# Attention with a mixture of experts on one core: five experts with an early block instead of four, gates by groups of query blocks, scaling by token tile, and weight maxima loaded expert by expert

## The chip, the cores and the metric

One core of a Trainium2 chip runs the whole program. The metric is the device time of one execution in microseconds (us); the kernel before is given by the median of three runs, and a profile of one further execution, with the start and length of every instruction, is what the prediction is argued from. PE is TensorE, DVE VectorE, ACT ScalarE, POOL GpSimd, SP SyncE, whose queue issues most transfers.

## The reference

Causal attention with a window of 128 over 8 batches, 8 heads, 576 positions and head size 64; its output, 4608 tokens of 512 numbers, goes through a mixture of 8 experts with noisy top-2 routing.

```python
mask = (rel >= 0) & (rel < window)                  # window = 128
scores = np.where(mask, scale * q @ k.T + slopes * -abs(rel), -1e9)
x = (softmax(scores) @ v)                           # rows: (batch, position), 512 wide
noisy = x @ w_gate + np.log1p(np.exp(x @ w_noise)) * noise
top2 = np.argpartition(-noisy, 2, axis=1)[:, :2]    # two experts per token, softmax weights
for e in range(8):
    for k in range(2):
        mask = top2[:, k] == e
        h = np.maximum(x[mask] @ w1[e], 0.0)        # 512 -> 1024
        out[mask] += top2_w[mask, k, None] * (h @ w2[e])   # 1024 -> 512
```

## The kernel before

**Precision.** Attention and the gate are computed in fp32. An expert's product is made of three products of rounded parts: high x high, high x low, low x high. In the first wave of expert blocks the parts are fp32r; in the second they are fp16, for which tokens and weights are first multiplied by a power of two that fits their largest absolute value, and the result is scaled back by `back`.

**Planner.** The order of the instructions on each engine is fixed while the program is written. Strands (Python generators) ask for an engine with an assumed duration and a rank, the due time; a small event simulation (`Order`) gives each engine, whenever it is free in the plan, the waiting step of the lowest rank. `either(a, b, rank, late, ...)` offers a step to ScalarE and, `late` us later, to VectorE. Buffers and PSUM banks are handed round in rings, also by rank. An `Event` holds a strand back in the plan; it is no semaphore of its own on the chip. `move` puts a transfer on SyncE's queue. The assumed durations and offsets at the top (`STAGE`, `LATE`, `GATE`, ...) steer the plan.

**Attention.** For each pair of heads (32) and each group of query blocks (`GROUPS`: blocks 0 and 1, blocks 2 and 3, the half block 4) a `unit` runs scores (L486 and L493), maxima with the bias on VectorE (L511), the exponential on ScalarE (L518), transposes (L530), their copies, and the product with the values (L561), whose result is copied to `xu`. When the four pairs of a batch are done, `rows` starts for each query block a `gate` (logits of gate and noise, L690, then the division by the softmax sums, L694, and the sum over heads, L699, on VectorE) and a `row_major` (L669, L672), which writes the tokens to `xs` in DRAM. `largest_value` takes the maximum of every value tile on VectorE (L455, L458, L459); since a token is a mean of values, one power of two from it (`xsc`) scales all tokens of the second wave.

**Routing.** `route(b)` follows batch by batch, one after the other: best two, their positions within each expert by products with triangular and all-one matrices (L746 to L750), a one-hot list of slots (L784, L790, product L794), and a scatter by GpSimd into the slot lists in DRAM (L870), for which `next_places` (L777) makes the row numbers `line_of`. For batches in `TIGHT` a chain of small steps is one planned step; for the others the last one-hot step may go to GpSimd.

**First wave.** After two batches (`CUTS`), the first 256 slots (`FIRST`) of experts 0 to 3 (`NF`) are filled, and their blocks run in fp32r between the attention steps: `weight` loads 256 KB pieces, casts them to the high part and subtracts for the low part (L988); `tokens` gathers the rows by GpSimd (L1059); `turn_tokens` transposes them; `ups` runs the up products (`mm1`, L1092) of a step (128 of the 1024 hidden columns), `middle` makes relu high part (L1112, L1114) and low part (L1129), `downs` the down products (`mm2`, L1140). The due times of the steps are spread evenly from `FFN0` to `FFN1`. Up products have one PSUM bank of their own (`hb`), shared with the routing's position products, down products two.

**Second wave.** When all units and all routes are done (`over`), attention's buffers are closed and the rest of each expert's slots runs in fp16: two blocks (512, 448) for the experts with a first block, three (512, 384, 320) for the others (`BLOCKS`). The last block of an expert has its down product flipped (L1145), so that the weights are the stationary side, and its result turned (L1200). `result` scales by the gate weight and scatters by GpSimd (L1219). Weights come through `scaled_weight` (L1044, L1048), which needs the expert's power of two; for experts 0 and 1 (`EARLY`) it comes from the rounded weights of the first wave (L992), for experts 2 to 7 `size_of_weights` loads each expert's weights once more in 512 KB pieces through three buffers (`mraw`, L1010) and reduces them (L1011), all six experts from the start of the second wave on, by rank.

After the planned part a loop over overflowing slots follows; the slots hold all tokens here, so it has no pass.

Of the kernel before, what the change touches and what calls it, by code (L numbers as in the profile page):

```python
# [22 lines left out]
NQ = 5  # L23
# [5 lines left out]
NF = 4  # L29
# [12 lines left out]
VALUES_LATE = 4.0  # L42
# [3 lines left out]
PLACES_LATE = 10.0  # L46
# [8 lines left out]
EARLY = 2  # L55
# [152 lines left out]
def attention_moe(ctx: ExitStack, tc: tile.TileContext, qk_, v, w_gate, w_noise, noise, w1, w2,  # L208
# [57 lines left out]
    ltr = ring(ap_, 2, [128, H, 16], F32, "lt")  # L266
# [37 lines left out]
    line_of = const.tile([E * SPAN, 1], I32, name="line_of")  # L304
    am = const.tile([128, 4], F32, name="am")
    mx = const.tile([128, 1], F32, name="mx")
# [3 lines left out]
    xmx = const.tile([128, 1], F32, name="xmx")  # L310
    xex = const.tile([128, 1], I32, name="xex")
    xsc = const.tile([128, 1], I32, name="xsc")
    xback = const.tile([128, 1], I32, name="xback")
    topped = Event()
# [27 lines left out]
    def set_ups():  # L342
# [19 lines left out]
        def columns():  # L362
# [6 lines left out]
            nc.vector.tensor_copy(line_of, first_line)  # L369
# [50 lines left out]
    def all_values():  # L420
        for y in range(2 * B):
# [30 lines left out]

    def largest_value(y, t, rank):
        def most(z, j, c):
            nc.vector.tensor_reduce(am[:, z:z + 1], t[:, j:j + c], axis=AX.XY, op=OP.max, apply_absolute_value=True)  # L455

        def all_():
            nc.vector.tensor_reduce(mx, am[:, 0:3], axis=AX.X, op=OP.max)  # L458
            nc.vector.tensor_tensor(xmx, xmx, mx, op=OP.max)  # L459

        for z, (j, c) in enumerate(((0, 2), (2, 2), (4, 1))):
            yield dve(0.34 if c == 1 else 0.6, rank, lambda: most(z, j, c))
        yield dve(0.14, rank, all_)
        if y == 2 * B - 1:
            spawn(powers_of_tokens())

    def powers_of_tokens():
        rank = FFN1 - 20
        a, wide = yield from of_all(xmx, 1, rank)

        def powers():
            floor_powers(xex, wide)
            nc.vector.tensor_scalar(xsc, xex, -1.0, float(256 << 23), op0=OP.mult, op1=OP.add)
            nc.vector.tensor_scalar(xback, xex, float(-2 << 23), None, op0=OP.add)

        yield dve(0.3, rank, powers)
        put(tb, a)
        put(turn_, 0)
        mark(topped)
# [93 lines left out]
    def unit(u):  # L573
# [45 lines left out]
        if g == NP - 1:  # L619
            spawn(rows(b, gr, t))  # L620
# [858 lines left out]
```

## Time and profile before

| what | value |
|---|---|
| runs | 1229.28, 1231.8, 1232.81 us |
| median | 1231.8 us |
| profiled execution, its own time | 1238.91 us |
| its span, first to last instruction | 1237.1 us |
| mean granted TensorE clock | 0.977 |
| second wave's first up product | at 450.3 us |
| weight pieces of 256 KB / maxima pieces of 512 KB | 192 / 48 loads |
| bytes moved by DMA | 169.13 MB |

A row of the profile's groups gives line, engine, operation, output and inputs with shapes, the count; then busy us of the group and mean ns of one; then the idle time of the engine just ahead of them and what ended it. The busy time of a group is the union of its instructions, so for pipelined products it is less than count times mean. Line numbers are those of the kernel above. A matmul in fp32 is recorded as two instructions.

### The profile page before, as it was taken

What the parts mean: (1) busy time and instruction counts of PE and PEld (TensorE: products, weight loads), DVE (VectorE), ACT (ScalarE), POOL (GpSimd) and SP (SyncE); (2) the same over time, 40 slices, a digit from 0 to 9 for tenths busy, and PEclk for the clock granted to TensorE, in tenths of its full rate; (3) what the DMA queues carried; (4) which work ended last, traced back from release to release, by engine and by line L of the source; (5) the groups of instructions that cost most, each with busy time, mean ns of one, the idle gap of its engine ahead of it and who ended that gap; (6) DMA issues with size and microseconds to landing.
All of it is one profiled execution on the core that took longest, in us unless ns stands there. A gap on an engine that the chain in (4) does not pass through costs nothing.

```text
span 1237.1 us, 20624 instructions
## 1 busy us (share of the span) xinstructions
PE 1165.7 (94%) x7447; PEld 722.2 (58%) x7447; DVE 694.4 (56%) x2108; ACT 518.6 (42%) x1365; POOL 292.3 (24%) x329
## 2 busy tenths in 40 slices
PE   7999799999997898999799999999999999999995
PEld 5776577778786763554454554555664564565552
DVE  7996789799988987665642432522351262242210
ACT  8775477676632352341331432332342251243211
POOL 5000101122224540320311331133221222322211
PEclk9998799999997999999999999999999999999998
DMA  8795445555244797885851651543451363342221
GB/s 266 279 308 192 136 121 162 159 157 131 58 133 125 230 293 244 251 232 163 246 124 31 142 124 25 147 86 61 90 134 30 53 174 61 61 112 43 35 26 22
DMA packets 132470, 169.13 MB, mean 137 GB/s; under 512 B 25360, under 2 KB 85008, under 8 KB 132368
## 3 DMA queue, kind: packets, MB, share of 16 engines
q1 hardware_dynamic: 114448, 127.48, 32.1%
q0 software_dynamic: 17920, 40.33, 17.7%
q8 instruction: 59, 0.97, 0.3%
q14 instruction: 43, 0.35, 0.1%
HBM read 126.38 MB, written 41.40 MB: 136 GB/s over the span
## 4 chain that ended last, share of the span: by engine, by line
PE 69%; DVE 10%; DMA 9%; issue 9%; ACT 2%; POOL 1%; SPq 0%; another core or an unknown queue 0%; POOLq 0%; DVEq 0%; ACTq 0%
PE bank L1092 26%; PE bank L1140 18%; PE bank L1145 8%; PE bank L561 3%; PE bank L530 3%; PE bank L493 3%; DMA raw<-in_w_dram 2%; PE bank L1072 2%; DMA out_dram<-yo,ix 2%; DVE p L511 2%; DMA slots_dram<-listed,line_of 1%; PE bank L690 1%; DVE wam L1011 1%; DMA xg<-xs_dram,ix 1%; DMA out_dram<-yo,ids 1%
## 5 line engine op out<-in xcount | busy, mean ns | idle before, releaser
L1129 DVE SCALAR_TENSOR_TENSOR bhl<-bank,bhh 128x512 f16<-128x512 f32 (+3 forms) x160 | 97.5, 610 | 334.6 <-ACT bhh L1112 320.8
L1219 POOL DMA_INDIRECT out_dram<-yo,ix x72 | 114.0, 1583 | 571.0 <-ACT yo L247 450.1
L1112 ACT ACTIVATE bhh<-bank 128x512 f16<-128x512 f32 (+3 forms) x146 | 78.7, 539 | 395.5 <-PE bank L1092 391.8
L1092 PE MATMUL bank<-bxh,w1hb 128*128 128x512 f16 (+3 forms) x640 | 222.3, 347 | 0.4 <-DMA xg<-xs_dram,ix 0.4
L1092 PE MATMUL bank<-bxl,w1hb 128*128 128x512 f16 (+3 forms) x640 | 222.1, 347 | 0.0
L1092 PE MATMUL bank<-bxh,w1lb 128*128 128x512 f16 (+3 forms) x640 | 222.1, 347 | 0.0
L1092 PEld LDWEIGHTS <-w1hb 128*128 128x128 f16 x1280 | 124.1, 98 | 104.3 <-issue 2.4
L1140 PE MATMUL bank<-w2hb,bhh 128*128 128x512 f16 (+1 forms) x376 | 142.8, 380 | 2.1 <-ACT bhh L1112 2.1
L1140 PE MATMUL bank<-w2hb,bhl 128*128 128x512 f16 (+1 forms) x376 | 142.5, 379 | 1.3 <-DVE bhl L1129 1.1
L1140 PE MATMUL bank<-w2lb,bhh 128*128 128x512 f16 (+1 forms) x376 | 142.5, 379 | 0.0
L518 ACT ACTIVATE p<-p,nm 128x256 f32<-128x256 f32 (+2 forms) x288 | 133.8, 469 | 10.1 <-DVE nm L511 9.5
L1140 PEld LDWEIGHTS <-bhh 128*128 128x128 f16 (+1 forms) x752 | 72.4, 98 | 82.8 <-issue 4.6
L511 DVE CUSTOM_DVE_ANT_0 p<-bank,bias 128x256 f32<-128x256 f32 (+2 forms) x288 | 95.3, 379 | 15.1 <-PE bank L493 10.6
L1092 PEld LDWEIGHTS <-w1lb 128*128 128x128 f16 x640 | 62.6, 98 | 55.0
L1082 DVE SCALAR_TENSOR_TENSOR bxl<-bank,xsc,bxh 128x512 f16<-128x512 f32 x72 | 51.6, 717 | 70.5 <-ACT bxh L247 55.5
L493 PE MATMUL bank<-qk 64*128 64x256 f32 (+1 forms) x512 | 72.0, 394 | 17.3 <-DVE nm L511 12.5
L530 PE MATMUL bank<-ident,p 128*128 128x128 f32 x512 | 83.2, 290 | 3.5 <-DVE pT L251 1.9
L561 PE MATMUL bank<-pT,vraw 128*64 128x128 f32 (+3 forms) x896 | 83.1, 309 | 1.3 <-DVE pT L251 0.7
L1059 POOL DMA_INDIRECT xg<-xs_dram,ix x72 | 72.7, 1009 | 23.9 <-issue 16.2
L1145 PE MATMUL bank<-bhh,w2hb 128*128 128x448 f16 (+1 forms) x224 | 74.5, 332 | 3.7 <-ACT bhh L1112 2.7
L247 ACT ACTIVATE pT<-bank 128x512 f32<-128x512 f32 (+1 forms) x115 | 56.6, 509 | 46.3 <-PE bank L530 41.8
L1145 PE MATMUL bank<-bhl,w2hb 128*128 128x448 f16 (+1 forms) x224 | 74.4, 332 | 1.0 <-DVE bhl L1129 1.0
(220 smaller groups left out, 1968.3 us busy)
## 6 DMA issues: line engine op xcount, KB each, us to landing
raw<-in_w_dram SPq DMA_DIRECT2D x192, 256.0 KB
mraw<-in_w_dram SPq DMA_DIRECT2D x48, 512.0 KB
qk<-in_qk_dram SPq DMA_DIRECT2D x32, 608.0 KB
out_dram<-xg SPq DMA_DIRECT2D x10, 1024.0 KB
vraw<-in_v_dram SPq DMA_DIRECT2D x16, 512.0 KB
xs_dram<-x SPq DMA_DIRECT2D x32, 256.0 KB
vraw<-in_v_dram SPq DMA_DIRECT2D x16, 128.0 KB
xg<-xs_dram,ix POOLq DMA_INDIRECT x72
```

The lines of the kernel that those rows point to most:

```text
L493: nc.tensor.matmul(s[h][:, o:o + c], qk[half, i * 128:i * 128 + 128], qk[half, QW + k0:QW + k0 + c], start=True, stop=True)
L511: nc.vector.tensor_tensor_reduce(out=p[:, z, h, 0:c], in0=s[h][:, o:o + c], in1=bv, scale=-0.125, scalar=3.0e38, op0=OP.add, op1=OP.min, a ...
L518: nc.scalar.activation(pv, pv, AF.Exp, bias=nm[:, z, h:h + 1], scale=-1.0, accum_out=den[:, z, 2 * g + h:2 * g + h + 1])
L530: nc.tensor.transpose(t[:, z], p[:, h, a:a + 128], ident)
L561: nc.tensor.matmul(o[half, o0:o0 + c], t[p0:128, kb, hh:hh + D], w, start=m == 0, stop=m == len(lst) - 1)
L1059: yield pool(1.04, rank, lambda: nc.gpsimd.indirect_dma_start(out=xg[0:r], out_offset=None, in_=xs[0:blk.rows], in_offset=bass.IndirectOff ...
L1092: nc.tensor.matmul(t[:, 0:blk.n], wp[:, c], x[:, c, 0:blk.n], start=c == 0 and z == 0, stop=c == 3 and z == 2)
L1112: nc.scalar.activation(o, i, AF.Relu)
L1129: yield dve(0.07 + c * 0.00104, rank - MIDDLE, lambda: nc.vector.scalar_tensor_tensor(hl[:, 0:c], t[:, 0:c], 0.0, high, op0=OP.max, op1=OP ...
L1140: nc.tensor.matmul(blk.y[j][0:r], h[:, cs], wp, start=f == 0 and m == 0, stop=f == 7 and m == 2)
L1145: nc.tensor.matmul(blk.y[c][:, 0:blk.n], wp[:, c * 128:c * 128 + 128], h[:, 0:blk.n], start=f == 0 and m == 0, stop=f == 7 and m == 2)
L1219: ins = nc.gpsimd.indirect_dma_start(out=out, out_offset=bass.IndirectOffsetOnAxis(ap=blk.ix[0:r, j:j + 1], axis=0), in_=t[0:r], in_offset ...
```

## The change

- `NF` 4 to 5: experts 0 to 4 get a first block of 256 slots; expert 4's second-wave blocks become (512, 448). `FFN0` and `FFN1`, between which the first wave's due times are spread, stay.
- `EARLY` 2 to 1: only expert 0's maxima come from the first wave. For experts 1 to 7 the 512 KB pieces are loaded, each expert's not before, in the plan, the previous expert's first second-wave block begins (`begun`).
- `largest_value`, `powers_of_tokens`, `xsc`, `xback` are gone; instead `fit` takes, for each gathered token tile of the second wave, the maximum per token, a power of two, scales the rows, and puts the inverse into the gate weights.
- `gate` works on a group: the four products have the 32 gate columns as stationary side and up to 256 tokens as moving side, each into 32 partitions of its own; the result is copied to SBUF (`gt`) and transposed back per block; the division and the sum over heads are one instruction each per group.
- `banks`: when all units are done (`attended`), and not the routes too, the two score banks go to the up products and one bank of the value product to the down products. The rest (one bank of `tb`) still waits for `over`.
- The slot list's place columns are ten small instructions with two per-partition operands in place of two large ones, always on VectorE; `line_of` has two buffers.

The diff, cut:

```diff
-NF = 4
+NF = 5
-EARLY = 2
+EARLY = 1
...
-            left["v", y] = 2 * len(GROUPS) + 1
+            left["v", y] = 2 * len(GROUPS)
             mark(valued[y])
-            yield from largest_value(y, t, rank + VALUES_LATE)
-            through(y)
...
-        done = Event(2 * nz)
+        done = Event(nz + 1)
+        spawn(gate(b, blocks, xus[b, gr], den, t, done))
...
-    def gate(b, i, xu, den, t, done):
+    def gate(b, blocks, xu, den, t, done):
...
             for c in range(4):
-                nc.tensor.matmul(a[0:rows, c * 32:c * 32 + 32], xu[:, c], wgn[:, c], start=True, stop=True)
+                nc.tensor.matmul(a[c * 32:c * 32 + 32, 0:c_], wgn[:, c], xu[:, c, 0:c_], start=True, stop=True)
-        yield pe(0.9, rank, logits)
+        yield pe(0.45 if nz == 2 else 0.15, rank, logits)
+        gt = yield (gtr, rank)
+        yield either(*((0.12, 0.13) if nz == 1 else (0.29, 0.33)), rank, LATE[2], lambda e: copy(
+            e, gt[:, 0:c_], a[:, 0:c_]))
...
+                nc.tensor.transpose(a2[0:rows, z * 128:z * 128 + 128], gt[:, z * 128:z * 128 + rows], ident)
...
-            V.tensor_add(line_of, tmp[0:m, 1, 0:1], first_line)
+            V.tensor_add(line_of[(b + 1) % 2], tmp[0:m, 1, 0:1], first_line)
...
+        def which_place(i):
+            for k in range(2):
+                V.tensor_scalar(hot[1][:, 2 * i + k], steps_[:, 0:LINE], d[:, i, k:k + 1], numbers[:, i:i + 1],
+                                op0=OP.is_equal, op1=OP.mult)
...
+    begun = [Event() for _ in range(E)]
     def size_of_weights(rg):
         for e in range(EARLY, E):
             done, rank = Event(8), SIZES[1] + step_of(e)
+            yield begun[e - 1]
...
+    def fit(blk, j, r, xg, rank):
+        m = yield (fitr, rank)
+        big, up_, down = (m[0:r, z:z + 1] for z in range(3))
...
+            V.tensor_mul(blk.gw[0:r, j:j + 1], xg[0:r, DM + blk.e:DM + blk.e + 1], down)
+        yield dve(0.6, rank, lambda: V.tensor_reduce(big, xg[0:r, 0:DM], axis=AX.X, op=OP.max, apply_absolute_value=True))
+        yield dve(0.7, rank, powers)
+        yield either(0.6, 0.6, rank, LATE[6], lambda e: copy(e, xg[0:r, 0:DM], xg[0:r, 0:DM], scale=up_))
...
     def ups(p, steps, ranks):
         for (blk, f), rank in zip(steps, ranks):
             if f == 0:
                 yield blk.ready
+                if p and begun[blk.e].count:
+                    mark(begun[blk.e])
...
+    def banks():
+        yield attended
+        for t in sb.free.pop():
+            put(hbr, t)
+        t = yield (ob, 0)
+        put(yb, t)
...
-        for r in (tb, ob):
-            t = yield (r, 0)
-            put(yb, t)
-        for t in sb.free.pop():
-            put(hbr, t)
+        t = yield (tb, 0)
+        put(yb, t)
```

More of the change, by code (lines that the diff above doesn't have):

```diff
@@ L41 @@
 VALUES = -12.4
-VALUES_LATE = 4.0
 GATE = (-41.8, -83.8)
@@ L303, in attention_moe @@
     tmp = const.tile([128, 2, E], F32, name="tmp")
-    line_of = const.tile([E * SPAN, 1], I32, name="line_of")
-    am = const.tile([128, 4], F32, name="am")
-    mx = const.tile([128, 1], F32, name="mx")
+    line_of = [const.tile([E * SPAN, 1], I32, name=f"line_of{z}") for z in range(2)]
     tops = const.tile([2, 1], F32, name="tops")
@@ L561, in weigh @@
                 nc.tensor.matmul(o[half, o0:o0 + c], t[p0:128, kb, hh:hh + D], w, start=m == 0, stop=m == len(lst) - 1)
-    over = Event(n + B)
+    over, attended = Event(n + B), Event(n)
     groups_ = range(len(GROUPS))
@@ L654, in attention_moe @@
     open_ = [Event() for _ in range(B + 1)]
-    gates = [Event(NQ) for _ in range(B)]
+    gates = [Event(len(GROUPS)) for _ in range(B)]
     routed = [Event() for _ in range(B)]
@@ L679, in row_major @@
         put(xr, x)
-    def gate(b, i, xu, den, t, done):
+    def gate(b, blocks, xu, den, t, done):
         rank = t - GATE[b + 1 in CUTS]
-        rows = 64 if i == 4 else 128
+        nz, i = len(blocks), blocks[0]
+        rows, c_ = (64, 64) if nz == 1 else (128, 256)
         yield set_up
@@ L857, in route @@
         spawn(gates_out(b, rank))
-        for c_, c2, f in hots:
-            if b in TIGHT or f is not number:
-                yield dve(c_, rank, lambda: f("DVE"))
-            else:
-                yield Op((("POOL", c2, rank), ("DVE", c_, rank + PLACES_LATE)), f)
+        yield dve(0.98, rank, which_line)
+        for i in range(NQ):
+            yield dve(0.28, rank, lambda: which_place(i))
         a = yield (tb, rank)
@@ L869, in scatter @@
             nc.gpsimd.memset(pad, 0.0)
-            nc.gpsimd.indirect_dma_start(out=slots, out_offset=bass.IndirectOffsetOnAxis(ap=line_of[:, 0:1], axis=0),
+            nc.gpsimd.indirect_dma_start(out=slots, out_offset=bass.IndirectOffsetOnAxis(ap=line_of[b % 2][:, 0:1], axis=0),
                                          in_=listed, in_offset=None, compute_op=OP.add)
@@ L942, in attention_moe @@
     second, lists2 = [], []
+    fitr = Ring([])
     chunks = {}
@@ L1030, in powers @@
             V.tensor_mul(back[:, e:e + 1], inv[:, 0:1], inv[:, 1:2])
-            V.tensor_mul(back[:, e:e + 1], back[:, e:e + 1], xback.bitcast(F32))
         yield dve(0.4, rank, powers)
@@ L1074, in turn_tokens @@
         yield pe(0.43, rank, turn)
-        yield either(0.16, 0.07, rank, 0.0, lambda e: copy(e, blk.gw[0:r, j:j + 1], xg[0:r, DM + blk.e:DM + blk.e + 1]))
+        if blk not in second:
+            yield either(0.16, 0.07, rank, 0.0, lambda e: copy(e, blk.gw[0:r, j:j + 1], xg[0:r, DM + blk.e:DM + blk.e + 1]))
         put(xgr, xg)
@@ L1259, in second_wave @@
         for z in range(4):
+            put(fitr, more.tile([128, 3], F32, name=f"fit{z}"))
+        for z in range(4):
             put(ixr, more.tile([128, 4], I32, name=f"ix{z}"))
         spawn(size_of_weights(ring(more, 3, [128, 1024], F32, "mraw")))
-        for r in (tb, ob):
-            t = yield (r, 0)
-            put(yb, t)
-        for t in sb.free.pop():
-            put(hbr, t)
+        t = yield (tb, 0)
+        put(yb, t)
         second.extend(Block(e, s0, c, NPAD, rings2) for e in range(E) for s0, c in BLOCKS[e >= NF])
@@ L1381, in attention_moe @@
     steps1 = [(blk, f) for blk in first for f in range(8)]
-    for strand in (loads(), masks(), all_values(), set_ups(), first_wave(), first_tokens(), second_wave(),
+    for strand in (loads(), masks(), all_values(), set_ups(), first_wave(), first_tokens(), banks(), second_wave(),
                    weights(0, lambda e, f: ranks1[8 * e + f] - WEIGHTS), last_weights(), all_powers(),
```

83 lines of the change are left out of this document (30 added, 53 removed).

## The prediction

> **What bounds the kernel now.** I read the page first (span, busy shares), then the stretches of 25 us, then the chain that ended last, and only then single groups and the order of time around the places that the change touches.
>
> ```profile
> span 1237.1 us, 20624 instructions
> PE 1165.7 (94%) x7447; PEld 722.2 (58%) x7447; DVE 694.4 (56%) x2108; ACT 518.6 (42%) x1365; POOL 292.3 (24%) x329
> ```
>
> TensorE is busy for 94% of the span, so the time is TensorE's work plus the holes in it. The stretches say where the holes are (columns: start and end, length, busy us and instruction count of PE, weight loads, VectorE, ScalarE and GpSimd, then the granted clock, DMA share and GB/s):
>
> ```profile
> 300.00:325.00 25.00, 24.23 (x234) 17.86 (x233) 22.36 (x105) 16.95 (x64) 4.05 (x4) 1.00 0.27 76
> 350.00:375.00 25.00, 23.37 (x195) 20.59 (x195) 21.02 (x86) 7.81 (x18) 7.64 (x8) 1.00 0.53 171
> 375.00:400.00 25.00, 17.01 (x99) 14.24 (x98) 21.12 (x66) 6.81 (x18) 10.67 (x11) 0.78 0.47 116
> 400.00:425.00 25.00, 22.93 (x129) 19.47 (x128) 22.41 (x46) 7.70 (x16) 12.47 (x14) 0.87 0.58 183
> 425.00:450.00 25.00, 19.52 (x114) 16.50 (x112) 21.95 (x39) 12.34 (x26) 13.62 (x13) 0.93 1.02 321
> 450.00:475.00 25.00, 20.66 (x99) 10.04 (x100) 20.35 (x39) 11.79 (x22) 6.87 (x7) 1.00 1.01 306
> 600.00:625.00 25.00, 18.77 (x91) 9.34 (x91) 16.58 (x34) 8.55 (x14) 1.65 (x3) 0.93 0.81 257
> 625.00:650.00 25.00, 23.46 (x127) 12.68 (x126) 9.72 (x18) 10.31 (x18) 6.38 (x7) 1.00 0.51 117
> 1075.00:1100.00 25.00, 25.00 (x159) 15.68 (x158) 7.33 (x13) 8.63 (x17) 8.12 (x8) 1.00 0.29 40
> ```
>
> Four stages stand out. Up to about 350 us attention runs with TensorE (24.2 of 25) and VectorE (22.4 of 25) both nearly full. From 350 to 475 the rest of the first wave of expert blocks runs while the last routes are computed: TensorE idles 1.6 + 8.0 + 2.1 + 5.5 + 4.3 = 21.5 us, the granted clock falls to 0.78, and VectorE is busy for 20 to 22 of every 25 us. The second wave has one hole, 6.2 + 1.5 us between 600 and 650, and from there runs as in the last row, at 25.00 of 25. So work removed from TensorE in the second wave comes off the time in full; work removed before 350 us comes off as far as VectorE lets it; and work on VectorE counts from 0 to 475 us alone.
>
> **The change part by part, 1: expert 4 in the second wave.** Its 1216 slots in three blocks (512, 384, 320) become 960 in two (512, 448), as experts 0 to 3 have them. The chain that ended last (start, length, what, count) repeats itself once per expert, and the same pieces give the period of each kind:
>
> ```profile
> 595.88 12.06 DMA raw<-in_w_dram
> ...
> 696.57 3.97 PE bank L1092 x21
> ...
> 780.58 3.97 PE bank L1092 x21
> ...
> 957.01 2.44 PE bank L1092 x15
> ...
> 1061.40 2.44 PE bank L1092 x15
> ```
>
> Two blocks take 780.58 - 696.57 = 84.0 us, three take 1061.40 - 957.01 = 104.4. TensorE has no idle time there, so this is **-20.4 us**, the surest term.
>
> **2: expert 4 in the first wave.** It adds eight steps of 12 up and 6 down products in fp32r.
>
> ```profile
> 358.86 0.40 PE L1140 MATMUL bank<-w2ha,ahh 128*128 128x512 f32 x1
> ...
> 359.55 0.28 PE L1092 MATMUL bank<-axh,w1ha 128*128 128x256 f32 x1
> ...
> 360.87 0.28 PE L1092 MATMUL bank<-axh,w1la 128*128 128x256 f32 x1
> 360.99 0.98 PE L690 MATMUL bank<-wgn,xu 128*128 128x32 f32 x8
> 361.80 0.64 PE L669 MATMUL bank<-ident,xu 128*128 128x128 f32 x4
> 362.19 0.48 PE L1140 MATMUL bank<-w2ha,ahh 128*128 128x512 f32 x1
> ```
>
> Starts follow starts, since products are pipelined: twelve up products take 360.99 - 359.55 = 1.44 us; three down products take 359.55 - 358.86 = 0.69, six 1.38. A step is 2.82 us, eight are 22.6, and the transposes of its two token tiles, by the four at 361.80 (0.39 each tile), 0.8: **+23.4 us**. They fall before 475 us. As idle time of 21.5 us exists there the term could be near 0; as the stage's own pace is slower than TensorE's it could be 41 (a rival below). Its weights are 16 more loads of 256 KB, and their rounding is ScalarE work (busy 7 to 12 of 25 us there) with the remainders split over GpSimd and VectorE.
>
> **3: the gate.** Forty calls of four fp32 products (two instructions each, all 128 columns of the array, 32 numbers moved) become 24 calls per group, whose four products each use 32 columns of the array, so that four can stand side by side, and move 256 numbers. Then come a copy, and a transpose per block.
>
> ```profile
> L690 PE MATMUL bank<-wgn,xu 128*128 128x32 f32 x256 | 32.8, 273 | 0.1
> L690 PE MATMUL bank<-wgn,xul 128*64 128x32 f32 x64 | 5.2, 225 | 0.0
> ```
>
> ```profile
> 347.84 1.09 PE L561 MATMUL bank<-pT,vraw 128*64 128x256 f32 x12
> 348.86 1.08 PE L690 MATMUL bank<-wgn,xu 128*128 128x32 f32 x8
> 349.87 0.60 PE L561 MATMUL bank<-pT,vraw 128*64 128x64 f32 x8
> ```
>
> ```profile
> 115.24 0.49 PE L486 MATMUL bank<-qk 128*128 128x192 f32 x2
> 115.57 0.60 PE L669 MATMUL bank<-ident,xul 128*64 128x128 f32 x4
> ```
>
> Removed: 38.0 us. No row shows 32 columns. On the whole array fp32 costs 0.33 us for 2 x 192 numbers, 0.86 ns each; the value product L561, on halves of 64 columns side by side, takes 1.02 us for its 12 instructions, by the code 4 of 256 and 8 of 128 numbers, 0.50 ns each: 1.7 times as fast with two abreast. A pair of blocks moves 8 x 256 = 2048 numbers: 1.76 us if nothing overlaps, 1.02 by the half array, 0.6 if the second halving again gives 1.7. I take 0.6, since halving is shown to pay. With 0.1 per transpose, 16 pairs cost 16 x 0.8 and 8 short groups about 8 x 0.3: 15 us. But the gate at 348.86, between value products on half arrays, took 1.01 us until the next start; that at 360.99, between work on the whole array, took 0.81. So going in and out of another shape costs 0.2, and 24 calls that now have a shape of their own 5 us. Gate: 15 + 5 - 38 = **-18 us**, bounds 0 (no overlap: 16 x 2.0 + 8 x 0.7 = 38) and -23 (no such cost).
> The Trainium skill, "TensorEngine Tiling (Array Packing)", section Tiling Modes, states that four 128x32 tiles work independently and that a change of mode drains TensorE, which speaks against small groups of them between whole-array work. The trace agrees for halves, by the 0.2 us; that four keep up a fourfold speed no row here shows, and by that speed the gate would be 3 us better than my term.
> On VectorE the gate's two operations go from 40 to 24 with twice the width, about even; the 24 copies mostly fall to ScalarE, not full in attention (16.95 of 25).
>
> **4: VectorE before 475 us.**
>
> ```profile
> L455 DVE TENSOR_REDUCE am<-vraw 128x1 f32<-128x512 f32 (+1 forms) x48 | 28.1, 588 | 0.0
> L992 DVE TENSOR_REDUCE wam<-w2ha 128x1 f32<-128x512 f32 x16 | 10.8, 675 | 0.0
> L992 DVE TENSOR_REDUCE wam<-w1ha 128x1 f32<-128x512 f32 x16 | 10.8, 674 | 0.0
> ```
>
> ```profile
> L1129 DVE SCALAR_TENSOR_TENSOR ahl<-bank,ahh 128x256 fp32r<-128x256 f32 x32 | 13.2, 412 | 4.9 <-ACT ahh L1112 4.4 <-issue 0.2
> ...
> L988 DVE TENSOR_TENSOR w2la<-raw,w2ha 128x512 fp32r<-128x512 f32 x15 | 12.7, 850 | 0.9 <-ACT w2ha L247 0.8
> ...
> L784 DVE TENSOR_TENSOR hot<-d,steps 128x640 f16<-128x640 f32 x8 | 6.5, 808 | 0.0
> ```
>
> ```profile
> L1011 DVE TENSOR_REDUCE wam<-mraw 128x1 f32<-128x1024 f32 x13 | 15.6, 1207 | 1.2 <-DMA mraw<-in_w_dram 1.2
> ```
>
> The last row is of 350 to 475 us alone. Gone: the maxima of the values (28.1), those of expert 1's rounded weights (half of 21.6), and 15.6 in the tail, held back with their 512 KB loads. That is 54 us off an engine that had 21 to 22 of 25. Added: a fifth expert's remainders, a quarter of 13.2 + 12.7, with its smaller shares some 10. The place columns of each batch's list become ten instructions on 64 elements in place of two on 640 (0.81 and about as much): ten of 0.08 to 0.2 (a tenth of 0.81, half of 0.41), even. All five experts share the due times that four had, so that more steps come up while attention runs. The score banks also go to the up products when attention ends and not when the last route has been sent, so that these no longer take turns on one bank. I take half of the tail's 21.5 us of idle time: **-11 us**; bounds -30 (all of it and the lost clock of 0.22, 0.13 and 0.07 of 25 us) and +5 (the first tiles of the second wave wait for their new scaling, ahead of a TensorE that is out of first-wave work).
>
> **5: the second wave's own new work.** Each of 70 token tiles gets a reduce (0.68, L992's shape), four small operations and a scaled copy before its transposes: some 2 us per tile, on VectorE (7.33 of 25) and ScalarE (8.63). Tokens have two sets of buffers and are fetched a block ahead, at the shortest 104.4 x 320 / 1216 = 27 us, which hides 4 x 2 us: 0. Without that cover it would be 8 us a block. The maxima of expert e are loaded once expert e-1 has begun. That wait is the planner's, while the program is written: it moves eight loads of 512 KB in SyncE's order, with weight loads queued behind them. At 306 GB/s (450 to 475 us) they take 14 us, with eight reduces of 1.2 beside them, in a period of 84; and the hole at 600 to 650, which the chain puts on a weight load of 12.06 us in this same queue, should go as the flood goes: **-6 us** of 7.7, bounds 0 and -7.7. The second line_of buffer can only take a wait away: 0.
>
> **Sum**: -20.4 + 23.4 - 18 - 11 - 6 = -32 us, on the profiled execution (span 1237.1, its own time 1238.91). The three runs have a median of 1231.8, 0.6% below that execution; the difference is carried over unchanged: **1200 us**. Bounds together: -20.4 + 23.4 + 0 + 5 + 0 = +8 to -20.4 + 23.4 - 23 - 30 - 7.7 = -58, 1240 to 1174.
>
> **Rivals.** *The tail keeps its pace (slower).* In 350 to 450 us there are 231 up products of fp32r, 19.3 steps, by
>
> ```profile
> 350.00:375.00 25.00, 6.98 (x44) 5.98 (x45) 1.00 0.53 171
> 375.00:400.00 25.00, 8.00 (x42) 7.64 (x40) 0.78 0.47 116
> 400.00:425.00 25.00, 11.67 (x79) 11.84 (x80) 0.87 0.58 183
> 425.00:450.00 25.00, 10.46 (x66) 9.57 (x65) 0.93 1.02 321
> ```
>
> (the same stretches, line of the up products alone): 5.2 us a step against TensorE's 2.8. If what sets that pace is the queue through cast, remainder and weight loads and not VectorE's load, eight more steps cost 41.6 and attention's savings turn into waiting: 41.6 - 20.4 - 6 = +15, 1247 us. It decides from a pace of 26.4 / 8 = 3.3 us on. Against it: VectorE and the banks are relieved just there. *Nothing but the move* (the 32-column tiles don't overlap, relief is not used): 23.4 - 20.4 - 6 = -3, 1229. *The tail is cleared*: all bounds of part 4 met, -51, 1181. *Held-back maxima come late*: a hole of 7.7 us for each of experts 1 to 7, +54 on the forecast, 1254; against it, 84 us for eight loads.
>
> **How the numbers follow.** Forecast 0.46, tail cleared 0.20, nothing but the move 0.15, tail keeps its pace 0.13, late maxima 0.06. A measurement of this kernel tells 0.3%, 3.7 us, from no change. Faster: 0.46 + 0.20 + half of 0.15 = 0.74; same: 0.07; slower: 0.13 + 0.06 = 0.19. The range, 1174 to 1238, holds the first three cases, 0.81; the likeliest alone would have 1187 to 1213.
>
> **What would show it.** Right: the two-block period of 84 us for expert 4; no hole in TensorE after the first second-wave product; the gate's TensorE time near 20 us; less than 15 us of TensorE idle between 350 us and that product, which begins before 450. Wrong: that product after 470, fp32r steps still above 3.3 us apart after attention, waits of TensorE on scaled weights or tokens at experts' starts, or gate products that follow each other at 0.2 us.

## The result and the profile after

| | before | after |
|---|---|---|
| median of 4 runs each (us) | 1232.3 (1229.28 to 1233.6) | 1212.16 (1209.84 to 1217.03) |
| profiled execution, its own time | 1238.91 | 1212.61 |
| span | 1237.1 | 1210.7 |

The ratio is 0.9844, 95% interval 0.9806 to 0.9882: 20 us faster, in the direction and the range forecast, 12 us short of the forecast 1200.

Three stretches of the span, cut at the first fp16 product and at 650 us, say where it went. The columns are those of the stretches in the prediction: length, busy us of PE, weight loads, VectorE, ScalarE, GpSimd, clock, DMA share, GB/s. First the kernel before:

```profile
0.00:450.26 450.26, 405.69 (x3332) 315.62 (x3333) 383.92 (x1536) 269.52 (x900) 106.47 (x118) 0.95 0.58 181
450.26:650.00 199.74, 186.71 (x948) 94.47 (x949) 127.20 (x224) 70.96 (x128) 45.77 (x51) 0.99 0.73 213
650.00:1224.18 574.18, 572.92 (x3169) 312.08 (x3166) 183.30 (x350) 177.06 (x337) 135.38 (x157) 1.00 0.36 77
```

and the changed kernel:

```profile
0.00:444.28 444.28, 403.56 (x3395) 302.75 (x3395) 372.29 (x1508) 279.65 (x926) 128.95 (x138) 0.98 0.61 187
444.28:650.00 205.72, 199.00 (x1020) 100.42 (x1020) 134.75 (x317) 78.79 (x130) 50.65 (x55) 1.00 0.61 169
650.00:1197.44 547.44, 539.33 (x2924) 286.88 (x2922) 268.90 (x659) 187.83 (x322) 126.47 (x146) 1.00 0.44 108
```

Length less PE's busy time is TensorE's idle time. The first stage is 6.0 us shorter, of which 3.9 is idle time (44.6 to 40.7) and 2.1 busy time. The second wave, last two rows together, is 20.8 us shorter, and all of it is busy time (759.6 to 738.3). Its idle time stays near 14 us, but it has moved: 13.0 us before 650 us became 6.7, and 1.3 us behind it became 8.1. What follows the last product is 0.3 us longer. Together -26.4 us of span.

The page of the changed kernel, and those of its 25 us stretches that answer to the ones shown before, with 525 and 700 us besides:

```profile
span 1210.7 us, 20898 instructions
PE 1142.3 (94%) x7336; PEld 690.1 (57%) x7336; DVE 775.9 (64%) x2483; ACT 547.3 (45%) x1378; POOL 310.7 (26%) x343
```

```profile
350.00:375.00 25.00, 22.17 (x173) 18.49 (x172) 22.41 (x75) 8.02 (x18) 10.50 (x10) 1.00 0.66 198
375.00:400.00 25.00, 18.92 (x122) 16.04 (x121) 20.08 (x50) 8.98 (x23) 15.35 (x14) 0.86 0.54 128
400.00:425.00 25.00, 19.89 (x132) 17.16 (x131) 24.41 (x56) 9.16 (x19) 15.73 (x15) 1.00 0.64 153
425.00:450.00 25.00, 21.85 (x121) 16.40 (x120) 22.36 (x55) 14.53 (x26) 16.24 (x14) 0.93 0.89 283
450.00:475.00 25.00, 22.58 (x108) 10.29 (x107) 21.77 (x51) 9.95 (x16) 2.58 (x2) 1.00 0.75 227
525.00:550.00 25.00, 23.32 (x121) 11.80 (x119) 17.45 (x40) 9.90 (x16) 9.36 (x11) 1.00 0.75 205
600.00:625.00 25.00, 25.00 (x136) 13.37 (x135) 15.26 (x25) 10.47 (x18) 4.16 (x5) 1.00 0.58 176
625.00:650.00 25.00, 22.93 (x114) 10.96 (x113) 17.33 (x49) 7.68 (x13) 5.22 (x7) 1.00 0.62 169
700.00:725.00 25.00, 23.34 (x119) 11.51 (x116) 19.59 (x47) 9.57 (x16) 9.38 (x11) 1.00 0.76 206
1075.00:1100.00 25.00, 25.00 (x168) 16.54 (x167) 16.39 (x44) 13.12 (x25) 5.94 (x7) 1.00 0.45 101
```

From 350 to 475 us TensorE still idles 19.6 us (21.5 before), VectorE is as full as it was, and GpSimd works more. The hole of 6.2 us at 600 is gone. In its place stand losses of 1.7 to 2.1 us at 525, 625 and 700, and so on: one near each expert's start.

### The profile page after: what moved, and what is told of

Read it like the earlier page. It is cut to its first block, busy times and chain, and to the rows that moved or that the text cites. A ratio compares the mean times of both kernels' runs of the same rounds, so it can differ in the third digit from the quotient of the medians.

```text
span 1210.7 us, 20898 instructions
## 1 busy us (share of the span) xinstructions
PE 1142.3 (94%) x7336; PEld 690.1 (57%) x7336; DVE 775.9 (64%) x2483; ACT 547.3 (45%) x1378; POOL 310.7 (26%) x343
## 4 chain that ended last, share of the span: by engine, by line
PE 58%; DVE 13%; DMA 8%; issue 4%; POOL 1%; ACT 0%; SPq 0%; POOLq 0%; another core or an unknown queue 0%; DVEq 0%
PE bank L1086 23%; PE bank L1136 16%; PE bank L1141 8%; DMA mraw<-in_w_dram 5%; PE bank L523 2%; PE bank L492 2%; DMA xg<-xs_dram,ix 2%; DVE wam L988 2%; PE bank L1066 2%; PE bank L455 2%; DVE hot L765 1%; POOL out_dram L1215 1%; DVE bxl L1076 1%; DVE fit L1051 1%; DMA raw<-in_w_dram 1%
## 5 line engine op out<-in xcount | busy, mean ns | idle before, releaser
L1086 PE MATMUL bank<-bxh,w1hb 128*128 128x512 f16 (+3 forms) x608 | 213.5, 351 | 0.0
L1086 PE MATMUL bank<-bxl,w1hb 128*128 128x512 f16 (+3 forms) x608 | 213.4, 351 | 0.0
L1086 PE MATMUL bank<-bxh,w1lb 128*128 128x512 f16 (+3 forms) x608 | 213.4, 351 | 0.0
L1086 PEld LDWEIGHTS <-w1hb 128*128 128x128 f16 x1216 | 118.0, 98 | 104.8 <-issue 1.9
L1136 PE MATMUL bank<-w2hb,bhl 128*128 128x512 f16 (+1 forms) x352 | 133.5, 379 | 4.2 <-DVE bhl L1125 4.2
L1136 PE MATMUL bank<-w2hb,bhh 128*128 128x512 f16 (+1 forms) x352 | 133.7, 380 | 0.6 <-ACT bhh L1108 0.5
L1136 PE MATMUL bank<-w2lb,bhh 128*128 128x512 f16 (+1 forms) x352 | 133.4, 379 | 0.0
L962 POOL TENSOR_TENSOR w1la<-raw,w1ha 128x512 fp32r<-128x512 f32 x35 | 48.7, 1392 | 161.9 <-ACT w1ha L245 115.2
L988 DVE TENSOR_REDUCE wam<-mraw 128x1 f32<-128x1024 f32 x56 | 67.7, 1211 | 19.9 <-DMA mraw<-in_w_dram 19.6
L1141 PE MATMUL bank<-bhh,w2lb 128*128 128x448 f16 (+1 forms) x224 | 75.5, 337 | 0.0
```

The lines of the kernel that those rows point to most:

```text
L988: yield dve(1.13, rank, lambda: nc.vector.tensor_reduce(o, t, axis=AX.X, op=OP.max, apply_absolute_value=True))
L1086: nc.tensor.matmul(t[:, 0:blk.n], wp[:, c], x[:, c, 0:blk.n], start=c == 0 and z == 0, stop=c == 3 and z == 2)
L1136: nc.tensor.matmul(blk.y[j][0:r], h[:, cs], wp, start=f == 0 and m == 0, stop=f == 7 and m == 2)
L1141: nc.tensor.matmul(blk.y[c][:, 0:blk.n], wp[:, c * 128:c * 128 + 128], h[:, 0:blk.n], start=f == 0 and m == 0, stop=f == 7 and m == 2)
```

## The experiments

**Theories.** Of the second wave: the new small holes come from held-back maxima (either because weight casts wait for the new scale, or because VectorE's queue stands at a maximum whose piece has not landed), or from the scaling of tokens, `fit`. Of the first: the fifth block costs what it takes on TensorE (23 us), or less because it fills idle time, or more because the stage keeps its pace; and what limits the stage after attention is the banks, the routing's place columns, or the way of the weights. Every edit makes the planner write another order on all engines, so a few us can come from that alone. A difference counts here only where the trace shows the wait that goes.

| kernel | median (us) | ratio to before, 95% |
|---|---|---|
| changed | 1212.16 | 0.9844, 0.9806 to 0.9882 |
| a_nf4: four first blocks | 1222.5 | 0.9892, 0.9848 to 0.9936 |
| b_nf5: before, five first blocks | 1252.07 | 1.0144, 1.01 to 1.0189 |
| a_gate: old gate | 1232.68 | 0.9992, 0.9967 to 1.0016 |
| b_gate: before, new gate | 1229.07 | 0.9967, 0.9945 to 0.9989 |
| a_late_banks: banks handed on late | 1220.75 | 0.9881, 0.9841 to 0.9921 |
| a_place: old place columns | 1211.93 | 0.9819, 0.9782 to 0.9855 |
| a_soon: maxima one expert earlier | 1210.89 | 0.9797, 0.9764 to 0.9831 |
| a_nofit: no scaling of tokens | 1219.22 | 0.9892, 0.9866 to 0.9918 |
| a_patient: reduces planned later | 1206.17 | 0.9768, 0.9734 to 0.9803 |
| a_lows: low parts off GpSimd | 1203.72 | 0.9741, 0.9708 to 0.9775 |
| a_patient_lows: both | 1195.12 | 0.9695, 0.9667 to 0.9723 |
| a_all: both, and lists planned later | 1185.32 | 0.9624, 0.9596 to 0.9652 |

The kernel before, run again beside these, has medians of 1233.8 to 1234.1 us, against 1232.3 beside the changed kernel, so 2 us between two rows mean nothing. A profile shows one run alone. Those of a_patient (1199.33), b_nf5 and a_all are of the fastest run, those of a_nf4 (1226.65), a_soon, a_nofit (1223.74), a_lows (1209.55) and a_patient_lows of the slowest. What a stretch of such a profile loses or gains need not be what the median does.

### The fifth block alone: a_nf4, b_nf5

```diff
-NF = 5
+NF = 4
```

> The changed kernel with four experts that have a first block, all else kept (expert 4 gets its three second-wave blocks back). Theory A, the fifth block is a swap: the second wave grows by 20.4 us and the first stage shrinks by TensorE's 23.4, so 1205 to 1215 us, no difference beyond 0.3%, and the whole gain of the change stands without it. Theory B, the first stage takes the fifth block in its idle time: the first stage stays near 444 us and the time is 1228 to 1233, the gain is the fifth block's.

The kernel before gets the opposite edit.

> The kernel before with five experts that have a first block and nothing else of the change. Theory A (a swap): the second wave shrinks by 20.4 us, the first stage grows by 23 or more, up to 41 at the tail's old pace of 5.2 us a step: 1232 to 1252. Theory B (idle time takes it): the first stage stays at 450 us and the time is about 1212.

In the changed kernel the fifth block gains 10 us (1222.5 to 1212.2); in the kernel before it costs 18 (1233.8 to 1252.1). The second wave answers alike: with four first blocks the changed kernel's second wave takes 777.6 us against 753.2, and the kernel before goes from 773.9 to 754.5 with five. The difference lies in the first stage. Here it is with four blocks in the changed kernel, with the stretch between the last fp32r product and the first fp16 one:

```profile
420.00:434.00 14.00, 4.95 (x19) 3.09 (x18) 12.43 (x33) 8.05 (x13) 6.11 (x7) 0.53 0.86 216
```

TensorE is out of first-wave work at 420.3 us and has only the second wave's token transposes until 434.2, with 9 of 14 us idle, while the second wave's tokens are being made ready. Five blocks fill that time: TensorE's busy time in the first stage rises by 19.5 us (384.1 to 403.6), its length by only 10.1 (434.2 to 444.3). In the kernel before the same block moves the first fp16 product from 450.3 to 479.5 and the last fp32r product from 452.6 to 487.5: 29 and 35 us for eight steps, 3.7 to 4.4 us a step. So the rival "the tail keeps its pace" is true of the kernel before: its fp32r up products behind 350 us follow at 5.3 us a step with five blocks (312 products, 26 steps, in 137 us) as at 5.4 with four. In the changed kernel the eight steps move the last fp32r product from 420.3 to 444.1 us, 3.0 a step, near TensorE's own 2.8. The other parts of the change together make this difference; which of them does is not shown.

### The gate: a_gate, b_gate

The kernel before's `gate`, one call per block, goes into the changed kernel:

```diff
-        spawn(gate(b, blocks, xus[b, gr], den, t, done))
         for z, i in enumerate(blocks):
+            spawn(gate(b, i, xus[b, gr][:, :, z * 128:z * 128 + nr], den[0:nr, z], t + z, done))
...
-                nc.tensor.matmul(a[c * 32:c * 32 + 32, 0:c_], wgn[:, c], xu[:, c, 0:c_], start=True, stop=True)
+                nc.tensor.matmul(a[0:rows, c * 32:c * 32 + 32], xu[:, c], wgn[:, c], start=True, stop=True)
```

> The changed kernel with the gate of before: forty calls of four products on the whole array, no copy, no transposes back. In the changed kernel the new gate's products took TensorE some 21 us with their transposes, the old ones 38. Theory A, attention is TensorE's, so the 17 us come back in full: 1222 to 1230. Rival, VectorE sets attention's pace and TensorE's saving was idle time: 1209 to 1216.

b_gate puts the new gate alone into the kernel before.

> The kernel before with the new gate alone: one call per group with four products on 32 columns each, copy, transposes. Undoing the gate took the whole gain from the changed kernel (1232.7). Theory A, TensorE's time in attention comes back whatever else the kernel has: 17 us, 1213 to 1220. Rival, the gain needs the relief of VectorE and the fifth block to be used, since routing ends no earlier: 1226 to 1235.

The rows of the gate in the changed kernel, L655 and L666 (the transposes) where the kernel before has its L690:

```profile
L655 PE MATMUL bank<-xu,wgn 128*32 128x256 f32 x128 | 10.6, 404 | 0.7 <-DVE x L635 0.7
L655 PE MATMUL bank<-xul,wgn 128*32 128x64 f32 x64 | 2.6, 231 | 0.0
L666 PE MATMUL bank<-ident,gt 128*128 128x128 f32 x32 | 6.3, 280 | 0.0
L666 PE MATMUL bank<-ident,gt 128*64 128x128 f32 x8 | 2.3, 282 | 0.0
```

Together 21.8 us against 38.0, and b_gate, where nothing else changes, has 17.2 us less busy TensorE in its first stage (388.5 against 405.7). Sixteen pairs take 10.6 us, 0.66 each (estimated 0.6), for 2048 numbers: 0.32 ns a number, against 0.86 on the whole array. That is 2.7 times as fast with four abreast. The same 17 us of TensorE are worth 4.9 us of time in the kernel before (1234.0 to 1229.1) and 20.5 in the changed one (1232.7 to 1212.2), where they go with the copies, banks and order that come with them. Of what the profile of a_gate is longer, 10.6 us lie in the first stage (first fp16 product at 454.9) and 8.1 in the second wave, where no gate runs: that share is the other order and not the gate. A part's worth is not a constant that can be added up.

### Banks and place columns: a_late_banks, a_place

```diff
         yield attended
-        for t in sb.free.pop():
-            put(hbr, t)
-        t = yield (ob, 0)
-        put(yb, t)
```

In a_late_banks these lines move back into `second_wave`, behind `over`.

> The changed kernel with the score banks and the spare bank handed on only when the last route has been sent, as before. Theory A, one bank for the up products is what held the first wave's pace after attention at 5.2 us a step (3.9 in the changed kernel): some 15 steps between 345 and 410 us at 1.3 us more, 10 to 20 us slower, 1222 to 1232. Rival, the relief of VectorE made that pace: within 0.4%, 1208 to 1217.

1220.75: the early banks are worth 8.6 us. The last fp32r product then comes at 450.0 instead of 444.1, and the second wave, whose idle time grows from 14.8 to 17.9, takes 5.4 us more. The pace that the expectation is about hardly moves: behind 350 us the fp32r steps are 4.6 us apart (259 up products), against 4.4 in the changed kernel (255 in 94 us; the 3.9 of the expectation counts products of the second wave too). So one bank for the up products can be only a small part of the old 5.2.

a_place puts the two old operations on 640 elements in place of the ten on 64:

```diff
...
-        for i in range(NQ):
-            yield dve(0.28, rank, lambda: which_place(i))
+        yield dve(0.75, rank, lambda: one_hot("DVE", 1))
+        yield dve(0.75, rank, lambda: number("DVE"))
```

> The changed kernel with the place columns of the slot list made by two instructions on 640 elements, as before, always on VectorE, in place of ten on 64. In the changed kernel the ten took 27.2 us of VectorE in all (80 of 388 ns); two of 0.81 and 1.0 us for 8 batches are 14.5. Theory A, VectorE sets the pace of the first stage's tail, where two of the eight lists are made and waits of TensorE on VectorE's remainders are 13 us: 2 to 5 us faster. Rival: it is hidden, within 0.3% of the changed kernel, 1209 to 1215.

1211.93, the same. The ten small operations cost more than estimated (388 ns each on average, 27.2 us for 80, estimated 0.08 to 0.2; the median is 293, some stand for GpSimd as shown below), but it shows nowhere in the time.

### The small holes: a_soon, a_nofit, a_patient

My first theory was the new scale: weight casts on ScalarE wait for it (27.2 us in six waits in the changed kernel). a_soon lets the maxima load one expert earlier:

```diff
-            yield begun[e - 1]
+            yield begun[max(e - 2, 0)]
```

> The changed kernel with each expert's weight maxima held back until the expert two before it has begun, not the one before (expert 2's follow expert 1's at once). Theory A: TensorE's idle time at the starts of experts 1 to 6, 11.8 us from 525 us on, comes from ScalarE's queue, which stands at a weight cast that needs the power of two, with the relu of the running block behind it; with the maxima a whole expert earlier this goes: 8 to 11 us faster, 1201 to 1204. Rival: the holes come from the scaling of the token tiles on VectorE and ScalarE: no change, 1210 to 1214, and holes at the same places.

The waits of the casts fall to 3.2 us, but the time is 1210.89, the second wave's idle time 14.2 us against 14.8, and the holes stand where they stood. The theory falls. a_nofit takes `fit` out (the tokens aren't scaled: that part of the computation is left out):

```diff
-        if blk in second:
-            yield from fit(blk, j, r, xg, rank)
...
```

> The changed kernel without the scaling of the second wave's token tiles: the maximum per token, the power of two, the scaled copy and the inverse in the gate weight are left out, tokens go to fp16 as they are. Theory A, this work (70 tiles of some 1.4 us on VectorE and 0.7 on ScalarE) is hidden, apart from the first tiles, which stand before the first fp16 product: 1206 to 1213. Rival, it makes the holes at the experts' starts: 1196 to 1203.

It is 7 us slower, 1219.22, with 765 us of second wave. So its absence gives nothing back here. But in that kernel transposes of tokens stand for 14.9 us behind result banks that ScalarE has not emptied; why the order came out so is not shown by any run, and so neither is what the absence of `fit` would give without that wait.

What holds TensorE is seen at one hole of the changed kernel, in order of time, first on VectorE, then on TensorE (start, length, what, in brackets the idle time ahead and what ended it):

```profile
545.61 1.22 DVE L988 TENSOR_REDUCE wam<-mraw 128x1 f32<-128x1024 f32 x1 [2.35 <-DMA mraw<-in_w_dram]
547.36 1.22 DVE L988 TENSOR_REDUCE wam<-mraw 128x1 f32<-128x1024 f32 x1 [0.53 <-DMA mraw<-in_w_dram]
548.50 0.68 DVE L1125 SCALAR_TENSOR_TENSOR bhl<-bank,bhh 128x512 f16<-128x512 f32 x1
```

```profile
547.18 0.38 PE L1136 MATMUL bank<-w2lb,bhh 128*128 128x512 f16 x1
549.24 0.39 PE L1136 MATMUL bank<-w2hb,bhl 128*128 128x512 f16 x1 [1.68 <-DVE bhl L1125]
```

VectorE works its queue in the order written. Two reduces stand there for pieces that have not landed, 2.35 and 0.53 us, and the low part `bhl` of the block that is running stands behind them; TensorE waits 1.68 us for it. By what ended them, TensorE's waits in the second wave of the changed kernel are these (total, times, longest):

```profile
PE bank L1136 <- DVE bhl L1125: 4.2, 4, 1.7
...
PE bank L1066 <- DVE bxl L1076: 3.0, 5, 1.6
...
PE bank L1066 <- ACT yo L245: 2.3, 2, 1.6
...
PE bank L1066 <- ACT xg L245: 2.2, 1, 2.2
...
PE bank L432 <- DVE bxl L1076: 1.5, 5, 0.4
```

So the low part `bhl` is 4.2 of the 14.8 us. As much, 4.5, are waits for `bxl`, the low part of the next tokens, out of the same queue of VectorE; the two longest of these (1.6 us at 891.7 and 0.9 at 998.3) stand behind reduces that had waited 2.27 and 1.69 us for their pieces. The rest is result banks that ScalarE has not emptied (2.3) and, once, at 459.6 us, tokens that `fit` has not scaled yet (2.2).

The plan lets the reduce follow its load too soon: a piece of 512 KB takes 6.6 us from issue to landing, by the last figure of this row of the transfers:

```profile
mraw<-in_w_dram SPq DMA_DIRECT2D x56, 512.0 KB, 6.6
```

a_patient has the plan wait 6 us more between load and reduce:

```diff
         yield from move(5.2e5, rank, lambda: nc.sync.dma_start(t, src))
+        yield order.now + 6.0
```

> The changed kernel with the plan told that a maxima piece lands 6 us later than it assumes, so that its reduce stands later in VectorE's order; nothing else. In the changed kernel VectorE stands at reduces whose pieces have not landed, 19.6 us in all, and the low part of the running block is queued behind them at each expert's start. Theory A, these are the holes of 11.8 us in the second wave: 6 to 10 us faster, 1202 to 1206. Rival, the holes come from the token tiles' scaling: no change, 1209 to 1214.

1206.17, and the second wave's idle time is 6.9 us (14.8). Its six runs spread from 1199.3 to 1209.6; the profile, of the fastest, has a span 13.2 us shorter where the median is 6.0 lower. VectorE's waits, of the changed kernel (total, times, longest) and, with one of TensorE, of a_patient:

```profile
DVE wam L988 <- DMA mraw<-in_w_dram: 19.6, 15, 2.4
```

```profile
DVE ix L885 <- DMA list<-slots_dram: 18.8, 6, 4.3
...
DVE wam L989 <- DMA mraw<-in_w_dram: 7.1, 4, 2.1
...
PE bank L1137 <- DVE bhl L1126: 5.0, 4, 1.4
```

The wait for pieces goes from 19.6 to 7.1 us, and another in the same queue takes part of its place: the numbers made from an expert's slot list, planned too soon behind their load. So TensorE's waits for `bhl` do not fall (4.2 to 5.0 us): all four now stand behind such a wait of VectorE, 3.3 to 4.3 us each. What went are those for `bxl` (4.5 us) and for the result banks (2.3); the second wave has neither any more.

### The way of the weights: a_lows, a_patient_lows, a_all

After attention, VectorE stands for several us within single small operations. One of them in the changed kernel, and what GpSimd does meanwhile:

```profile
381.09 0.20 DVE L788 TENSOR_TENSOR l<-l,noi 128x40 f32<-128x40 f32 x1
381.32 6.16 DVE L789 TENSOR_TENSOR l<-l,lg 128x40 f32<-128x40 f32 x1
387.40 0.68 DVE L1079 TENSOR_TENSOR axl<-bank,axh 128x512 fp32r<-128x512 f32 x1
```

```profile
381.85 1.88 POOL L962 TENSOR_TENSOR w2la<-raw,w2ha 128x512 fp32r<-128x512 f32 x1
383.10 1.88 POOL L962 TENSOR_TENSOR w1la<-raw,w1ha 128x512 fp32r<-128x512 f32 x1
384.34 1.86 POOL L962 TENSOR_TENSOR w2la<-raw,w2ha 128x512 fp32r<-128x512 f32 x1
385.58 1.83 POOL L962 TENSOR_TENSOR w1la<-raw,w1ha 128x512 fp32r<-128x512 f32 x1
```

An operation like the 0.20 us one ahead of it takes 6.16, until the last of four back-to-back subtractions of weights on GpSimd ends (385.58 + 1.83 = 387.4). The next down product on TensorE had waited 5.12 us at 390.29 for a low part out of this queue. Summed over VectorE's instructions from 320 to 445 us, what each takes above the median of its operation and shape makes some 24 us. a_lows gives these subtractions to VectorE alone for experts 3 and 4, whose weights come in this stage:

```diff
-        yield Op((("POOL", 1.23, rank), ("DVE", 0.6, rank + WEIGHTS_LATE)),
+        yield Op((("POOL", 1.23, rank), ("DVE", 0.6, rank + WEIGHTS_LATE)) if e < 3 else (("DVE", 0.6, rank), ("DVE", 0.6, rank)),
```

> The changed kernel with the low parts of the first-wave weights of experts 3 and 4 all on VectorE, none on GpSimd. In the changed kernel VectorE operations of 0.2 us took up to 6.2 us while GpSimd made low parts back to back, 26.6 us above their usual lengths from 320 to 445 us, and TensorE waited 13.3 us there for the low part of the hidden values. Theory A, the two engines shut each other out: the excess falls to below 10 us, VectorE gains more than the some 20 operations of 0.68 us it takes over, and the first fp16 product comes before 440 us: 1204 to 1210. Rival, VectorE is full there and the moved work is paid: the first fp16 product after 448, 1216 to 1228.

1203.72, and the first fp16 product comes at 433.6 instead of 444.3. Groups of VectorE from 320 to 445 us, changed kernel, then a_lows:

```profile
L962 DVE TENSOR_TENSOR w2la<-raw,w2ha 128x512 fp32r<-128x512 f32 x9 | 7.5, 828 | 1.1 <-ACT w2ha L245 1.1
L789 DVE TENSOR_TENSOR l<-l,lg 128x40 f32<-128x40 f32 x2 | 6.3, 3174 | 0.0
L1298 DVE TENSOR_SCALAR bias<-bias 1x8 int32<-1x8 int32 x1 | 4.9, 4870 | 0.0
```

```profile
L962 DVE TENSOR_TENSOR w2la<-raw,w2ha 128x512 fp32r<-128x512 f32 x19 | 14.0, 737 | 0.3 <-ACT w2ha L245 0.3
...
L789 DVE TENSOR_TENSOR l<-l,lg 128x40 f32<-128x40 f32 x2 | 0.4, 195 | 0.0
L1298 DVE TENSOR_SCALAR bias<-bias 1x8 int32<-1x8 int32 x1 | 0.2, 158 | 0.0
```

VectorE has more work, 21 more subtractions of `w1la` and `w2la` of some 0.7 us, and is done earlier, since 3.17 and 4.87 us shrink to 0.2, and the 24 us above the medians to 8. TensorE's waits there for the low part `ahl` fall from 13.3 to 4.5 us. The edit frees GpSimd too, which gathers the tokens, but TensorE's waits for gathered tokens there do not fall (1.0 to 2.6 us). Of the 10.7 us won in the first stage this profile, of the slowest of six runs, loses 8.1 again in the second wave (761.3 us against 753.2, idle 20.2), where the small holes still stand; as the median is 8.4 us below the changed kernel's, other runs presumably lose less. The next kernel has both edits, this one and a_patient's.

> The changed kernel with both edits that paid: reduces of the maxima planned 6 us later, and the low parts of experts 3 and 4 on VectorE alone. Theory, the two holes are apart (second wave and first stage): the first fp16 product near 434 us as with the second edit alone, 742 us from there as with the first alone, 13 us of tail: 1188 to 1194. Rival, the earlier second wave meets new late loads and gives one of the two back: 1200 to 1206.

1195.12: 17 us below the changed kernel, against 6 and 8.4 for the single edits. In its profile the waits for the lists, and TensorE's for `bhl`, are larger than in a_patient:

```profile
DVE ix L885 <- DMA list<-slots_dram: 22.0, 6, 5.0
...
PE bank L1137 <- DVE bhl L1126: 8.5, 7, 2.1
```

a_all has the plan wait 4 us more for these lists:

```diff
             yield from move(1e4, rank, load_ids)
+            if q:
+                yield order.now + 4.0
             yield dve(0.3, rank, numbers_)
```

> As the kernel with both edits, and the plan told that the slot lists of the second wave's blocks (all but the first) land 4 us later than it assumes: with the first edit alone VectorE stood 18.8 us at the numbers made from these lists. Theory, most of that has the low part of a running block behind it, and 2 to 5 us more are gained: 1184 to 1190. Rival, nobody waits for VectorE there: the same as without, within 0.3%.

1185.32, the best here: ratio 0.9624 (0.9596 to 0.9652), 2.2% below the changed kernel. Its stretches:

```profile
428.51:650.00 221.49, 217.83 (x1105) 109.59 (x1105) 142.69 (x336) 83.26 (x137) 51.72 (x61) 0.99 0.60 164
650.00:1169.00 519.00, 518.47 (x2838) 279.78 (x2837) 266.69 (x648) 181.22 (x311) 122.99 (x143) 1.00 0.46 114
```

TensorE idles 4.2 us in the whole second wave, 0.5 of them behind 650 us. VectorE's waits for the lists are gone, and TensorE's for `bhl` are 0.7 us, once.

## Why the prediction was right, and where not

**By stage.** The terms of the first stage, +23.4 - 18 - 11, made -5.6 us; it became 6.0 shorter. Those of the second wave, -20.4 - 6, made -26.4; it became 20.8 shorter. The span was forecast at -32 and came to -26.4. What is missing is the second wave's idle time, forecast 6 shorter and 0.5 longer; the other terms give 0.9 of that back. That the first stage's sum is right is luck, as two of its errors cancel (below).

**Expert 4 in the second wave (-20.4): right.** Busy time fell by 21.3. The chain of the changed kernel shows the period of two blocks stretched by the small holes:

```profile
506.61 3.97 PE bank L1086 x21
592.93 3.97 PE bank L1086 x21
679.41 3.97 PE bank L1086 x21
```

86.3 and 86.5 us instead of the forecast 84.0; a_all, without the holes, has 83.6 (577.75 to 661.33 in its chain).

**Expert 4 in the first wave (+23.4): right as work, less as time.** TensorE's busy time rose by 19.5 against a_nf4, the time by 10, because the second wave could not begin earlier anyway. The prediction counted 21.5 us of idle time there as a reason for a bound near 0 and then took no cover; in the changed kernel, by a_nf4, about half was covered. In the kernel before nothing was (b_nf5).

**The gate (-18): right**, -16.2 by the rows, -17.2 in b_gate. The Trainium skill's "TensorEngine Tiling (Array Packing)", section Tiling Modes, has four 128x32 tiles work independently; 2.7 times as fast as the whole array agrees with that in kind. The same section states that a change of mode drains TensorE; what that costs these rows do not separate.

**VectorE before 475 us (-11 of idle time): this step failed in its size, and another stood in for it.** The idle time fell by 3.9 only. VectorE was to lose some 44 us of work (54 off, 10 added); its busy time up to the first fp16 product fell by 11.6. Some of that is the place columns, 27.2 us for what two rows of the prediction put at about half, yet a_place shows that they cost no time. What did cost time is that VectorE's busy time there is in part waiting for GpSimd, as the 6.16 and 4.87 us show; the prediction read "20 to 22 of every 25 us" as work. The profile of the kernel before, counted as above, already has 17 us of it, as one operation at two places shows:

```profile
376.90 2.76 DVE L764 SCALAR_TENSOR_TENSOR ef<-ef,d 128x10 f32<-128x10 f32 x1
...
403.10 0.17 DVE L764 SCALAR_TENSOR_TENSOR ef<-ef,d 128x10 f32<-128x10 f32 x1
```

The first ends at 379.66, with the second of two subtractions on GpSimd (379.62). The prediction also put the weights' remainders down to a share "split over GpSimd and VectorE" with no price for doing them on GpSimd. That the stage's sum still came out is luck: TensorE's busy time fell by 2.1 where +23.4 - 18 would have it rise by 5.4. The mean granted clock in the stage rose from 0.95 to 0.98, and 3% of 405 us would be 12 us, so it could be the clock. But in b_gate it rose to 0.97, and the busy time fell by no more than 17.2, of which the gate's own rows make 16. No run isolates it, and the cause stays open.

**Held-back maxima (-6): the old hole went, and new ones of the same sum came; this term failed.** Idle time up to 650 us fell by 6.3, as forecast, and rose by 6.9 behind it. The prediction asked only whether SyncE's queue and VectorE had room for eight loads and reduces in 84 us, and they have. It did not ask what stands behind a reduce that waits in VectorE's queue. The rival "held-back maxima come late" had the right place, an expert's start, and the wrong size: 1.3 to 2.6 us lost around each, instead of 7.7. The paragraph on what would show it named waits on scaled weights or tokens; one such wait came, 2.2 us for scaled tokens at 459.6, and the others are on low parts, of the running block (4.2) and of the next tokens (4.5), and on result banks (2.3). Of its other signs, the first fp16 product before 450 us (444.3) and a gate near 20 us (21.8) came true; less than 15 us of idle time ahead of that product (94.28 - 77.11 = 17.2 us from 350 on), no hole behind it and fp32r steps below 3.3 us apart (4.4) did not.

**`fit` (0): not refuted**, as its absence gave nothing back; TensorE waits for its scaled tokens once in the second wave, 2.2 us.

**From the profiled execution to the median.** "The difference is carried over unchanged" failed: the profiled execution of before was 7.1 us above the median used, that of after 0.5 above its own. This makes 6.6 of the 12.4 us by which the forecast, 1199.8 before rounding, missed; the 5.6 of span and 0.1 of rounding and ends make the rest. A single profiled execution is one draw (the runs of the kernel before beside the experiments went from 1227.1 to 1243.5), and its distance from the median is no property of the kernel.

**The rivals.** "The tail keeps its pace" decides from 3.3 us a step. In the changed kernel 255 up products between 350 us and the last fp32r product, 21.3 steps in 94 us, are 4.4 us a step, beyond the point given. Yet the kernel became faster, since part of those steps covers time that a_nf4 spends idle: the point from which it decides was set as if nothing else held the second wave's start.

## What to carry to other kernels

In a program whose order is fixed beforehand, an operation that waits for a transfer blocks everything written behind it on its engine: plan it at the transfer's measured landing time, which gave back 6 and 10 us here, with a line or two each. A busy engine is not a working one; compare single long instructions with others of the same line and shape before counting their time as load that can be taken off. And price added work against the next thing that its stage waits for: the same fifth block cost 18 us in one kernel and gained 10 in another, and the gate gave 5 in one and 20, order and all, in the other.

## What the hardware showed that was not expected

- VectorE and GpSimd: a 128x40 tensor-tensor operation on VectorE, 0.20 us otherwise, took 6.16 us across four GpSimd subtractions, and one of 1x8 int32 with a single input took 4.87 us (0.16 in a_lows) across three (410.77 to 414.9 us). The Trainium skill's "SBUF — State Buffer", section "SBUF: two separate sides", states that the two engines share a pair of ports which one of them holds for a whole instruction, for VectorE's operations with two inputs in SBUF among others. The trace agrees in that each of the two ends with a subtraction (387.4 and 414.9 us). It shows more than one instruction's wait: VectorE did not get in between the four, which start 1.25 us apart.
- Four fp32 products on 32 columns each, side by side, move a number in 0.32 ns, against 0.50 for two on halves and 0.86 on the whole array.
- `tensor_scalar` with two per-partition operands on 128x64 fp16 took 293 ns in the median (388 on average, with waits for GpSimd), where four times as many elements, 128x256 in fp32 from a bank, took 412 ns; the estimate by elements, 80 to 200 ns, was too low.
